# Local-attention blocks of 63 keys, v in one transfer a head, narrower pooling matmuls and pooled q and k on GpSimd

## The chip, the cores and the metric

The kernel runs on one core of one Trainium2 chip. The metric is device time in microseconds: the median of several executions. Before the change it is 880.45 us over 3 runs (879.81 to 880.62).

## The reference

Four batches of eight heads, 576 positions of 64 elements each, go through two attentions whose results are added: one over q, k and v averaged by fours (144 positions, its output repeated four times), and one on full resolution in which a position sees only the positions closer than 4. The sum is laid out as 2304 tokens of 512 and goes through two feed-forward layers of width 2048.

```
q_d, k_d, v_d = mean over groups of 4 positions
out_up  = repeat(softmax(q_d k_d^T / 8) v_d, 4)
mask    = |i - j| < 4
out_loc = softmax(where(mask, q k^T / 8, -1e9)) v
x = (out_up + out_loc) as (2304, 512)
h = x @ w_in;   x = (h * sigmoid(h)) @ w_out
h = x @ w_in2;  out = elu(h) @ w_out2
```

## The kernel before

All matmuls are float32 or pairs of rounded halves; a product of two matrices in the feed-forward layers is three matmuls (high by high, high by low, low by high).

The program has two stages. In the first, the attention of 16 head pairs (`attend`, a batch is four pairs) is interleaved with the first half of the first layer on blocks of 256 tokens (`unit`: lines 1124 and 1172). In the second (`paired`), the rest of both layers runs as matmuls of lines 1500, 1588 and 1590, with the instructions back to back on TensorE.

The order of the first stage is made by a planner in the program text: a `Job` has an engine, a planned duration, predecessors, buffers that it takes (`Slots`, `Hold`) and a due time; `pick` emits the job that can start earliest by the planner's clocks. The constants near line 56 (`D_LOCAL`, `S_LOCAL`, `STICK`, `T_FIRST`, `clock_of` and so on) are its prices. Every engine then executes its own list in that fixed order and waits on semaphores. Where the planner sees TensorE without work, `fill` puts in dummy matmuls (line 370).

For one head pair, `attend` does this. SyncE loads rows of q and k (line 604), TensorE turns them (line 653), ScalarE or VectorE copies them out (lines 681 to 687). Local attention takes ten blocks of 64 queries against 64 keys (line 773), masks, exponentiates and normalises them (`across`, on GpSimd line 784 or VectorE), turns them (line 900) and multiplies with v (line 1005). The windows of v come from `load_windows`: the first nine blocks start 57 rows apart and come in one transfer a head (line 614), the tenth starts at S - 64 and comes in a second (line 618). Pooled attention sums q and k by fours on VectorE (line 695), multiplies (line 847), exponentiates (line 869), normalises (line 886), turns (line 921) and multiplies with pooled v (line 939). Pooled v is made on TensorE for batch 0 (line 708, 22 matmuls a pair against a 0/1 matrix in `natv`), and for the other batches from another load of v (line 608) on GpSimd (lines 727, 728) or VectorE (line 732). Line 1022 adds both attentions into x.

The 16 weights of the first stage (8 slices of w_in, 8 of w_out, 512 KB each) come over SyncE's queue (lines 395, 400) into three buffers and one lent one. Each is decoded from its 64-bit input form on ScalarE (lines 426, 430) and VectorE (lines 434, 437, 441), and then split on ScalarE (line 1101) and GpSimd (line 1105). A buffer is free for the next weight when line 441 is done.

The last rows of the output are scaled and added on VectorE (line 1553) and stored by SyncE (line 1560).

Of the kernel before, what the change touches and what calls it, by code (L numbers as in the profile page):

```python
# [15 lines left out]
ALU = mybir.AluOpType  # L16
# [6 lines left out]
def attention_moe_moe2_kernel(ctx, tc, q, k, v, wi1, wo1, wi2, wo2, out):  # L23
# [32 lines left out]
    PACKED, PE_POOLED, HALVED, CHUNKED, STICK, T_SECOND = 0, 1, 0, 4, 3, 40.0  # L56
    STICK_FROM = 0
    BACKLOG = 3.0
    D_ROWS, D_LOCAL, D_V, D_W, S_ROWS, S_LOCAL, X_AFTER = 1.6, 1.9, 1.5, 2.2, 1.1, 2.2, 1
# [5 lines left out]
    SLACK, MOST_H, N_PSUM, SPLIT_F = 0.05, 2, 16, 3  # L65
    T_MM, T_FIRST, T_PAIR = 0.1185, 38.0, 6.4
# [10 lines left out]
    w0 = [57 * i for i in range(NW - 1)] + [S - WIN]  # L77
# [3 lines left out]
    for i in range(NW):  # L81
        lo, hi = a0[i], a0[i + 1] - 1
        assert q0[i] <= lo and hi < q0[i] + WIN
        assert w0[i] <= max(lo - 3, 0) and min(hi + 3, S - 1) < w0[i] + WIN
    WF_N, WS_N = 3, 3

    LENT = {'rows': [(5, 1), (6, 0), (6, 1)], 'ws': [(7, 0)], 'v': [(7, 1)]}
# [37 lines left out]
    def constants():  # L125
# [3 lines left out]
        for n, (half, low, high) in enumerate([(0, 0, 6), (0, -3, 3), (1, 0, 6), (1, -3, 3)]):  # L129

            for sign, bound in ((1, -low), (-1, high)):
                nc.gpsimd.affine_select(
                    out=tmp[:, n, :], in_=tmp[:, n, :], compare_op=ALU.is_ge, fill=MASKED,
                    base=bound + sign * WIN * half, pattern=[[sign, WIN]], channel_multiplier=-sign,
                )
        for s in range(NW // 2):
# [15 lines left out]
    clock_of = {"A": 0.0, "V": 4.0, "G": 4.0, "S": 0.0, "P": 5.0, "dma": 0.0, "port": 4.0}  # L152
# [357 lines left out]


    POOLED_BY = [(w, 0) for w in range(NW // 2 + 1)] + [(w, 1) for w in range(NW // 2, NW)]

    def pooler():
        return natv[:, :len(POOLED_BY) * HS].rearrange("p (n m) -> p n m", m=HS)

    def pool_matrix():

        m = pooler()
        nc.gpsimd.memset(m[:WIN], 1.0)  # L520
        for n0, n1 in ((0, NW // 2 + 1), (NW // 2 + 1, len(POOLED_BY) - 1), (len(POOLED_BY) - 1, len(POOLED_BY))):
            w, c = POOLED_BY[n0]
            x = m[:WIN, n0:n1]
            for sign, base_ in ((1, 0), (-1, FAC - 1)):
                nc.gpsimd.affine_select(
                    out=x, in_=x, compare_op=ALU.is_ge, fill=0.0, base=base_ + sign * (w0[w] - FAC * HS * c),
                    pattern=[[sign * w0[1], n1 - n0], [-sign * FAC, HS]], channel_multiplier=sign,
                )
        nc.vector.tensor_copy(m[WIN:P], m[:WIN])

    def pool_rows(w):

        return min(w0[1], w0[w + 1] - w0[w]) if w < NW - 1 else WIN
# [15 lines left out]
    )  # L549
    QKD0 = Slots([xb[:, c, :2 * SD] for c in range(NPAIR)])  # L550
# [28 lines left out]
    def attend(i, due):  # L579
# [5 lines left out]
        by_pe = b < PE_POOLED  # L585
# [24 lines left out]
        def load_windows():  # L610
            vw = hw.tile.rearrange("p (n d) -> p n d", d=D)
            for j in range(2):
                rows = v[b, h0 + j]
                nc.sync.dma_start(
                    vw[j * WIN:(j + 1) * WIN, :NW - 1, :],
                    bass.AP(tensor=rows.tensor, offset=rows.offset, ap=[[D, WIN], [w0[1] * D, NW - 1], [1, D]]),
                )
                nc.sync.dma_start(vw[j * WIN:(j + 1) * WIN, NW - 1, :], rows[w0[-1]:w0[-1] + WIN, :])
# [21 lines left out]
        copies = []  # L640
        prior = []
        for n_, cells in enumerate(([(0, c) for c in range(NTB - 1)], [(1, c) for c in range(NTB - 1)], [(0, NTB - 1), (1, NTB - 1)])):
# [21 lines left out]
            for which in range(2):  # L664
                n = TB * sum(w == which for w, _ in cells)
                if n:
# [17 lines left out]
                    else:  # L684
# [3 lines left out]
                        )  # L688
                    copies.append(alike(0.19 + 0.0008 * n, ops[0], 0.15 + 0.00106 * n, ops[1], [pj], uses=[bank]))
# [3 lines left out]
        def pool_qk():  # L693
            for which, src in enumerate(hqk.tile):
                nc.vector.reduce_sum(hqkD.tile[:, which * SD:(which + 1) * SD], src.rearrange("p (m r) -> p m r", r=FAC), axis=AX.X)

        red = Job("V", 1.48, pool_qk, copies, takes=[hqkD], uses=[hqk])
        vd = lambda: hvd.tile.rearrange("p (n d) -> p n d", n=4)
        pv = []
        if by_pe:  # L700
            bankv = [Hold(banks, "a") for _ in range(2)]

            def pool_v():
                vw = hw.tile.rearrange("p (n d) -> p n d", d=D)
                for n, (w, c) in enumerate(POOLED_BY):
                    for j in range(2):
                        rows_ = slice(j * WIN, j * WIN + pool_rows(w))
                        nc.tensor.matmul(  # L708
                            bankv[j].tile[:HS, c * D:(c + 1) * D], pooler()[rows_, n, :], vw[rows_, w, :],
                            start=n == 0, stop=n == len(POOLED_BY) - 1, skip_group_check=True,  # L710
                        )

            psv = Job("P", 0.85, pool_v, [lw], lat=0.2, takes=bankv, uses=[hw, hpool], mode="d")
            for j in range(2):
                dst = lambda j=j: hvd.tile[:HS, 2 * j * D:2 * (j + 1) * D]
                pv.append(alike(
                    0.29, lambda dst=dst, j=j: nc.scalar.copy(dst(), bankv[j].tile[:HS, :2 * D]),
                    0.29, lambda dst=dst, j=j: nc.vector.tensor_copy(dst(), bankv[j].tile[:HS, :2 * D]),
                    [psv], takes=[hvd] if j == 0 else [], uses=[bankv[j]],
                ))  # L720
            pv[1].after(pv[:1])
# [31 lines left out]
        for part, (s0, s1, halves_, outs) in enumerate(parts):  # L753
# [6 lines left out]
            def scores(s0=s0, s1=s1, held=held):  # L760
# [9 lines left out]
                for w in range(2 * s0, 2 * s1):  # L770
                    o, c = (w % 2) * WIN, (w // 2 - s0) * WIN
                    for j in range(2):
                        nc.tensor.matmul(  # L773
                            held[j].tile[o:o + WIN, c:c + WIN],
                            qT[j * D:(j + 1) * D, q0[w]:q0[w] + WIN],
# [979 lines left out]
```

## Time and profile before

| | |
|---|---|
| median of 3 runs | 880.45 us |
| profiled execution | 879.63 us |
| its span | 877.9 us |
| TensorE busy (matmuls) | 865.9 us, 99% |
| VectorE | 668.7 us, 76% |
| ScalarE | 543.7 us, 62% |
| GpSimd | 251.5 us, 29% |
| bytes moved | 100.08 MB, mean 114 GB/s |

The span is what the profile covers; the execution's own time is 1.7 us longer. Busy shares are means over two unlike stages, so the stages are read apart.

### The profile page before, as it was taken

How to read it: one execution, taken by the hardware profiler on the slowest of the kernel's cores; microseconds unless marked ns; L12 is line 12 of the kernel's file. 1: busy time of each engine (PE TensorE's matmuls, PEld its weight loads, DVE VectorE, ACT ScalarE, POOL GpSimd, SP SyncE). 2: the span in 40 equal slices, each digit the busy share in tenths (PEclk: the TensorE clock that was granted, in tenths of full speed). 3: DMA queues.
4: the chain of work that ended last, by engine and by line, in shares of the span. 5: the costliest groups of instructions: out<-in, count | busy, mean ns of one | idle time of the engine just before them, and what ended most of it. 6: DMA issues, size and time to landing. Idle time of an engine off the chain costs nothing.

```text
span 877.9 us, 17291 instructions
## 1 busy us (share of the span) xinstructions
PE 865.9 (99%) x6632; PEld 809.7 (92%) x6640; DVE 668.7 (76%) x1255; ACT 543.7 (62%) x1228; POOL 251.5 (29%) x269
## 2 busy tenths in 40 slices
PE   8989999999999999999999999999999999999998
PEld 5779989999999999999999998898998998998986
DVE  8888777776968988979569879389489797493552
ACT  5787675564568568466377387385586684561750
POOL 4488786664103011301024213010141041010000
PEclk9989999999999999999999999999999999999999
DMA  9996377612123436253521340541420531310301
GB/s 170 205 219 173 81 202 180 169 49 97 56 90 121 132 103 221 77 173 125 178 92 52 109 156 1 166 123 60 132 72 37 174 126 37 111 70 37 108 0 72
DMA packets 105522, 100.08 MB, mean 114 GB/s; under 512 B 62240, under 2 KB 92448, under 8 KB 105312
## 3 DMA queue, kind: packets, MB, share of 16 engines
q1 hardware_dynamic: 103072, 98.39, 38.1%
q8 instruction: 52, 0.85, 0.4%
q10 hardware_dynamic: 2368, 0.59, 0.4%
q14 instruction: 30, 0.25, 0.1%
HBM read 75.37 MB, written 23.59 MB: 113 GB/s over the span
## 4 chain that ended last, share of the span: by engine, by line
PE 94%; DVE 2%; DMA 2%; issue 1%; ACT 0%; SPq 0%; POOL 0%; ACTq 0%; POOLq 0%; DVEq 0%
PE b L1500 33%; PE b L1590 22%; PE b L1588 15%; PE b L1172 8%; PE b L1124 7%; PE b L653 1%; PE b L1005 1%; PE b L921 1%; PE b L939 1%; PE b L900 1%; PE b L773 1%; PE b L847 1%; PE b L708 1%; DMA rows<-in_k_dram 1%; DMA ws<-in_moe_w_out_dram 1%; DMA rows<-in_q_dram 1%
## 5 line engine op out<-in xcount | busy, mean ns | idle before, releaser
L1590 PE MATMUL b<-w,grw 128*128 128x512 f32 x384 | 121.2, 389 | 0.0
L1590 PE MATMUL b<-w,ghk 128*128 128x512 f32 x288 | 99.1, 389 | 0.0
L1500 PE MATMUL b<-xhr,xaw 128*128 128x384 f32 x360 | 96.4, 335 | 0.0
L1588 PE MATMUL b<-grw,w 128*128 128x384 f32 x352 | 91.2, 334 | 0.0
L1590 PEld LDWEIGHTS b<-w,grw 128*128 128x128 f32 x384 | 72.1, 188 | 14.9
L1500 PE MATMUL b<-xhr,w 128*128 128x384 f32 x320 | 83.8, 335 | 0.0
L1124 PE MATMUL b<-xh,w 128*128 128x256 f32 x384 | 82.5, 293 | 1.2 <-DVE t L1153 0.7
L1172 PE MATMUL b<-gh,w 128*128 128x256 f32 x384 | 79.6, 288 | 0.0
L1590 PE MATMUL b<-w,glk 128*128 128x512 f32 x192 | 74.8, 389 | 0.0
L1588 PE MATMUL b<-ghk,w 128*128 128x384 f32 x248 | 71.6, 334 | 0.0
L1124 PEld LDWEIGHTS b<-xh,w 128*128 128x128 f32 x384 | 64.7, 194 | 3.0 <-DVE t L1153 0.9
L1500 PE MATMUL b<-xlr,xaw 128*128 128x384 f32 x200 | 66.9, 334 | 0.0
L1500 PEld LDWEIGHTS b<-xhr,xaw 128*128 128x128 f32 x360 | 65.5, 188 | 0.0
L1590 PEld LDWEIGHTS b<-w,ghk 128*128 128x128 f32 x288 | 54.1, 188 | 11.1
L1172 PEld LDWEIGHTS b<-gh,w 128*128 128x128 f32 x384 | 63.3, 191 | 0.7 <-ACT t L1152 0.2
L1588 PEld LDWEIGHTS b<-grw,w 128*128 128x128 f32 x352 | 63.7, 188 | 0.0
L1512 ACT COPY hg<-b 128x384 f32<-128x384 f32 x60 | 28.7, 480 | 52.5 <-PE b L1500 51.9
L1553 DVE SCALAR_TENSOR_TENSOR part<-b,part 128x384 f32<-128x384 f32 (+1 forms) x42 | 25.0, 609 | 44.8 <-PE b L1590 28.4
L1283 DVE TENSOR_TENSOR xlr<-tail,xhr 128x768 fp32r<-128x768 f32 x51 | 49.6, 973 | 11.5 <-ACT xhr L1280 11.2
L1500 PEld LDWEIGHTS b<-xhr,w 128*128 128x128 f32 x320 | 58.0, 188 | 0.2
L1588 PE MATMUL b<-glk,w 128*128 128x384 f32 x168 | 56.1, 334 | 0.0
L1280 ACT CAST xhr<-tail 128x768 fp32r<-128x768 f32 x60 | 50.0, 834 | 7.0 <-DVE tail L1361 4.3
(259 smaller groups left out, 2380.8 us busy)
## 6 DMA issues: line engine op xcount, KB each, us to landing
ws<-in_moe_w_in_dram SPq DMA_DIRECT2D x32, 512.0 KB
ws<-in_moe_w_out_dram SPq DMA_DIRECT2D x31, 512.0 KB
tail<-x SPq DMA_DIRECT2D x24, 384.0 KB
x<-part SPq DMA_DIRECT2D x6, 768.0 KB
out_dram<-part SPq DMA_DIRECT2D x18, 256.0 KB
vw<-in_v_dram SPq DMA_DIRECT2D x28, 144.0 KB
tail<-xd SPq DMA_DIRECT2D x10, 384.0 KB
natv<-in_v_dram SPq DMA_DIRECT2D x22, 144.0 KB
```

The lines of the kernel that those rows point to most:

```text
L653: nc.tensor.transpose(bank.tile[:, n * TB:(n + 1) * TB], row(which, c)[:TB], ident[:TB, :TB])
L708: nc.tensor.matmul(bankv[j].tile[:HS, c * D:(c + 1) * D], pooler()[rows_, n, :], vw[rows_, w, :], start=n == 0, stop=n == len(POOLED_BY) - ...
L773: nc.tensor.matmul(held[j].tile[o:o + WIN, c:c + WIN], qT[j * D:(j + 1) * D, q0[w]:q0[w] + WIN], kT[j * D:(j + 1) * D, w0[w]:w0[w] + WIN], ...
L1124: nc.tensor.matmul(ph.tile[:, :NB0], w[a][:, c, :], x_slot(n, c, b_), start=start and m == 0, stop=stop and m == len(products) - 1,)
L1172: nc.tensor.matmul(y[d // 2].tile[:, o:o + NB0], w[m // 2][:, sl], gg(m % 2), start=f == 0 and m == 0 and d % 2 == 0, stop=fin and m == 2, ...
L1280: a = Job("A", ACT_[width], lambda: nc.scalar.copy(hi(), src), preds, gate)
L1283: other=("V", VEC_[width], lambda: nc.vector.tensor_tensor(lo(), src, hi().bitcast(F32), ALU.subtract)),
L1500: nc.tensor.matmul(acc_, a[:, cs], b[:, c, :], start=fresh and c == 0 and m == 0, stop=c == 1 and m == 2, skip_group_check=True,)
L1512: snap[after, j] = [Job("A", ACT_[NB], lambda dst=dst, acc_=acc_: nc.scalar.copy(dst, acc_), [], gate, due=soon)]
L1553: nc.vector.scalar_tensor_tensor(dst, src, sc, dst, op0=ALU.mult, op1=ALU.add)
L1588: nc.tensor.matmul(y[d][:, :NB], wm[:, sl], gm, start=first, stop=last_)
L1590: nc.tensor.matmul(y[d], gm[:, sl], wm, start=first, stop=last_)
```

## The change

A block of local attention now counts 63 keys (it had 64), and all ten blocks start 57 rows apart, so that v comes in one transfer a head. The last block has 63 key columns; its 64th score column is masked, and in batches 1 to 3 a matmul of one column more per head fills it. The 0/1 matrix for pooling v becomes 128 by 128, with v as the weights: ten matmuls a head with 14 to 16 columns, one copy, two transposes and one copy. It is used for the first seven pairs and not four. For batch 0, q and k are summed by fours in two additions each (`pool_twice`), for which the planner may take GpSimd or VectorE. The lent row buffers go. The very last output block is computed, scaled and stored in two halves of 256 columns, the second store from ScalarE's queue. Several planner constants change.

```diff
-    PACKED, PE_POOLED, HALVED, CHUNKED, STICK, T_SECOND = 0, 1, 0, 4, 3, 40.0
+    PACKED, PE_POOLED, HALVED, CHUNKED, STICK, T_SECOND = 0, 7, 0, 4, 2, 40.0
-    D_ROWS, D_LOCAL, D_V, D_W, S_ROWS, S_LOCAL, X_AFTER = 1.6, 1.9, 1.5, 2.2, 1.1, 2.2, 1
+    POOL_G = 1
+    D_ROWS, D_LOCAL, D_V, D_W, S_ROWS, S_LOCAL, X_AFTER = 1.6, 2.5, 1.9, 2.7, 1.1, 1.3, 1
-    SLACK, MOST_H, N_PSUM, SPLIT_F = 0.05, 2, 16, 3
-    T_MM, T_FIRST, T_PAIR = 0.1185, 38.0, 6.4
+    SLACK, MOST_H, N_PSUM, SPLIT_F = 0.05, 3, 16, 3
+    T_MM, T_FIRST, T_PAIR = 0.1185, 36.0, 6.4
-    w0 = [57 * i for i in range(NW - 1)] + [S - WIN]
+    KEYS = WIN - 1
+    w0 = [(KEYS - 6) * i for i in range(NW)]
-    LENT = {'rows': [(5, 1), (6, 0), (6, 1)], 'ws': [(7, 0)], 'v': [(7, 1)]}
+    LENT = {'ws': [(7, 0)], 'v': [(7, 1)]}
...
-    clock_of = {"A": 0.0, "V": 4.0, "G": 4.0, "S": 0.0, "P": 5.0, "dma": 0.0, "port": 4.0}
+    clock_of = {"A": 0.0, "V": 4.0, "G": 4.0, "S": 0.0, "P": 3.0, "dma": 0.0, "port": 4.0}
...
-        by_pe = b < PE_POOLED
+        by_pe = i < PE_POOLED
...
                 nc.sync.dma_start(
-                    vw[j * WIN:(j + 1) * WIN, :NW - 1, :],
-                    bass.AP(tensor=rows.tensor, offset=rows.offset, ap=[[D, WIN], [w0[1] * D, NW - 1], [1, D]]),
+                    vw[j * WIN:j * WIN + KEYS],
+                    bass.AP(tensor=rows.tensor, offset=rows.offset, ap=[[D, KEYS], [w0[1] * D, NW], [1, D]]),
                 )
-                nc.sync.dma_start(vw[j * WIN:(j + 1) * WIN, NW - 1, :], rows[w0[-1]:w0[-1] + WIN, :])
...
+        def pool_twice(which):
+            x = hqk.tile[which].rearrange("p (m r) -> p m r", r=FAC)
+            z = half_sums[which].rearrange("p (m r) -> p m r", r=2)
+            nc.gpsimd.tensor_tensor(z, x[:, :, 0:2], x[:, :, 2:4], ALU.add)
+            nc.gpsimd.tensor_tensor(
+                hqkD.tile[:, which * SD:(which + 1) * SD].rearrange("p (m o) -> p m o", o=1), z[:, :, 0:1], z[:, :, 1:2], ALU.add
+            )
...
-                for n, (w, c) in enumerate(POOLED_BY):
+                for w in range(NW):
+                    m0, m1 = pg[w], pg[w + 1]
                     for j in range(2):
-                        rows_ = slice(j * WIN, j * WIN + pool_rows(w))
                         nc.tensor.matmul(
-                            bankv[j].tile[:HS, c * D:(c + 1) * D], pooler()[rows_, n, :], vw[rows_, w, :],
-                            start=n == 0, stop=n == len(POOLED_BY) - 1, skip_group_check=True,
+                            bankv.tile[j * D:(j + 1) * D, m0:m1], vw[j * WIN:j * WIN + KEYS, w, :],
+                            pooler[j * WIN:j * WIN + KEYS, j, FAC * m0 - w0[w], :m1 - m0], start=True, stop=True, skip_group_check=True,
                         )
...
+            def turn_v():
+                for c in range(2):
+                    nc.tensor.transpose(bankt.tile[:HS, c * P:(c + 1) * P], hvt.tile[:, c * HS:(c + 1) * HS], ident)
...
+                        if final and k == FP - 1 and d == ny - 1:
+                            for c0, queue in ((0, nc.sync), (DM // 2, nc.scalar)):
...
-            prepare(i, dues[pos] - 2.5 if which == 0 else dues[pos + LAG] - 2.5)
+            prepare(i, dues[pos] - 4.0 if which == 0 else dues[pos + LAG] - 4.0)
```

The lists of the engines change in many places. Two of them matter here. The first is SyncE's list from the end of the loads of v windows for batch 0 on (`vw` and `yo` are buffers of windows, `ws` and `lent` of weights, `nat` and `lent` of q, k and v rows). Before:

```order
L614 DMA yo<-in_v_dram 64x9x64
L618 DMA yo<-in_v_dram 64x64
L400 DMA ws<-in_moe_w_out_dram 128x1024
L395 DMA ws<-in_moe_w_in_dram 128x4x256
L400 DMA lent<-in_moe_w_out_dram 128x1024
L604 DMA lent<-in_q_dram 96x6x64 x2
L604 DMA lent<-in_k_dram 96x6x64 x2
L608 DMA lent<-in_v_dram 72x512 x2
L395 DMA ws<-in_moe_w_in_dram 128x4x256
```

and with the change, from the first weight on:

```order
L399 DMA ws<-in_moe_w_in_dram 128x4x256
L609 DMA vw_116<-in_v_dram 63x10x64 x2
L609 DMA vw_117<-in_v_dram 63x10x64 x2
L609 DMA yo<-in_v_dram 63x10x64 x4
L404 DMA ws<-in_moe_w_out_dram 128x1024
L399 DMA ws<-in_moe_w_in_dram 128x4x256
L404 DMA lent<-in_moe_w_out_dram 128x1024
L399 DMA ws<-in_moe_w_in_dram 128x4x256
L599 DMA nat_113<-in_q_dram 96x6x64 x2
L599 DMA nat_114<-in_k_dram 96x6x64 x2
```

Eight transfers of v windows stand where sixteen stood, the fifth weight (the third w_in) has moved ahead of the rows of pair 4, and no load of v (line 608) stands here any more.

The second is GpSimd's list after it has built its constants (`ring` and `yo` hold scores, `tail` and `xa` turned q and k, `xb` their sums). Before, up to the first split of a weight:

```order
L784 TENSOR_TENSOR ring_118<-ring_118,small 128x640
L886 TENSOR_TENSOR ring_120<-ring_120,small 72x576
L784 TENSOR_TENSOR ring_119<-ring_119,small 128x640
L886 TENSOR_TENSOR yo<-yo,small 72x576
L784 TENSOR_TENSOR yo<-yo,small 128x640
```

and with the change, its start:

```order
L694 TENSOR_TENSOR natv<-tail 128x288
L695 TENSOR_TENSOR xb<-natv 128x144
L807 TENSOR_TENSOR ring_118<-ring_118,small 128x640
L909 TENSOR_TENSOR ring_120<-ring_120,small 72x576
L694 TENSOR_TENSOR natv<-xa 128x288
L695 TENSOR_TENSOR xb<-natv 128x144
L807 TENSOR_TENSOR ring_119<-ring_119,small 128x640
```

The two rows of line 694 and 695 stand four times ahead of the first normalisation (q and k of pairs 0 and 1), twice between pair 0's and pair 1's, and twice more for pair 3: all eight sums of batch 0 are on GpSimd, in line with the normalisations.

## Rows read from the trace of the kernel before

**Rows 1.** Stretches of 20 us: busy time (count) by engine, TensorE clock, DMA share, GB/s.
```profile
0.00:20.00 20.00, 17.60 (x243) 11.42 (x248) 16.32 (x43) 11.25 (x36) 8.46 (x27) 1.00 1.04 178
40.00:60.00 20.00, 17.57 (x255) 15.05 (x256) 17.60 (x37) 16.14 (x43) 14.21 (x17) 0.83 0.89 190
80.00:100.00 20.00, 20.00 (x209) 19.18 (x207) 15.24 (x30) 14.55 (x39) 12.86 (x15) 1.00 0.37 107
```
**Rows 2.** Waits of TensorE: line and what it waited for, us in total, times, longest.
```profile
PE b L370 <- issue: 2.0, 3, 1.6
PE b L653 <- DMA nat<-in_q_dram: 1.9, 2, 1.6
PE b L1124 <- DVE t L1153: 0.7, 1, 0.7
PE b L1124 <- DVE wf L441: 0.5, 1, 0.5
```
**Rows 3.** Stretches of 1 us, columns as in rows 1.
```profile
53.00:54.00 1.00, 1.00 (x26) 0.78 (x28) 1.00 (x2) 0.96 (x5) 0.90 (x3) 0.50 1.11 333
59.00:60.00 1.00, 1.00 (x10) 0.95 (x9) 0.90 (x6) 1.00 (x3) 0.73 (x1) 0.87 0.57 141
```
**Rows 4.** Chain that ended last, in order of time: start us, us, what.
```profile
258.50 23.97 PE b L1500 x138
872.98 2.05 DVE part L1553 x3
```
**Rows 5.** TensorE in order of time: start us, us, line, tiles, count [idle before <-releaser].
```profile
1.39 3.92 PE L370 MATMUL b<-t 128*128 128x512 bf16 x10 [1.39 <-DVE t L1614]
5.67 0.60 PE L653 MATMUL b<-ident,nat 96*128 96x96 f32 x5 [0.36 <-DMA nat<-in_q_dram]
6.11 1.03 PE L370 MATMUL b<-t 128*128 128x512 bf16 x4
9.28 0.75 PE L773 MATMUL b<-tail 64*64 64x64 f32 x40
12.98 1.21 PE L653 MATMUL b<-ident,rows 96*128 96x96 f32 x12
28.67 1.65 PE L708 MATMUL b<-yo,natv 57*72 57x64 f32 x44
63.29 0.28 PE L1124 MATMUL b<-xh,w 128*128 128x256 f32 x1
```
**Rows 6.** SyncE's queue in order of time.
```profile
11.68 0.73 SPq L614 DMA_DIRECT2D vw<-in_v_dram  x1
24.12 0.64 SPq L618 DMA_DIRECT2D yo<-in_v_dram  x1
25.43 0.43 SPq L395 DMA_DIRECT2D ws<-in_moe_w_in_dram  x1
873.70 1.69 SPq L1560 DMA_DIRECT2D out_dram<-part  x3
```
**Rows 7.** VectorE in order of time.
```profile
8.54 1.41 DVE L695 TENSOR_REDUCE xb<-tail 128x144 f32<-128x576 f32 x2
49.76 0.41 DVE L1153 SCALAR_TENSOR_TENSOR t<-t,b 128x256 f32<-128x256 f32 x1
57.33 0.69 DVE L441 SCALAR_TENSOR_TENSOR wf<-ws,b 128x512 int32<-128x512 int32 x1
```
**Rows 8.** GpSimd groups with shapes: count | busy us, mean ns of one | idle before.
```profile
L784 POOL TENSOR_TENSOR ring<-ring,small 128x640 f32<-128x640 f32 x27 | 34.0, 1260 | 29.1 <-DVE small L879 13.9 <-DVE small L830 8.2 <-DVE small L816 7.0
L728 POOL TENSOR_TENSOR vd<-natv 72x128 f32<-72x128 f32 x17 | 7.8, 457 | 2.1 <-PE b L939 0.9
L1070 POOL TENSOR_TENSOR xl<-xa,xh 128x256 fp32r<-128x256 f32 x16 | 11.5, 731 | 1.3 <-ACT xh L1066 1.3
```

**Rows 9.** GpSimd in order of time.
```profile
30.85 1.15 POOL L886 TENSOR_TENSOR ring<-ring,small 72x576 f32<-72x576 f32 x1 [2.25 <-DVE small L880]
```
**Rows 10.** DMA over 0 to 80 us in 40 slices of 2 us.
```profile
GB/s 6 219 202 213 214 215 216 260 133 105 86 119 135 227 383 299 203 221 204 172 166 135 143 232 262 193 291 143 225 112 321 223 274 224 173 224 207 134 134 322
```

## What was predicted

> **What bounds the kernel now.** I read the stretches of time first, then the waits of TensorE, the chain that ended last, and then each engine's list in order of time over the first 66 us. From 80 us on TensorE is busy in every stretch, and the chain is a run of back-to-back matmuls from 258.50 to 872.98 [rows 1, 4]. Those 614.5 us are the same matmuls after the change, so only three things can move: the start, the work that the first stage gives TensorE, and the end. In the start the reader should see TensorE 2.4 us short of each of two 20 us stretches, with VectorE at 16.3 and 17.6 of 20 [rows 1]; waits for rows of q (1.9 us), for issue (2.0), for a decoded weight (0.5) and for a VectorE result (0.7) [rows 2]; and seven slices, 53 to 60 us, in which the granted clock is between 0.50 and 0.87, so at the lower level of 1.2 GHz for most of them, after TensorE had waited for q at 50.7 to 52.3 [rows 2, 3]. The last of the four first-layer units of batch 0 that I take as a milestone (48 matmuls of line 1124) ends at 63.4 [rows 5]. From there to 258.50 are **195.1 us** in which TensorE hardly waits. The question is when the changed kernel passes the same milestone, and how much work it then has left.
>
> **TensorE's work.** The old pooling of v is 22 matmuls in 1.57 us, 0.071 each; 88 of them are 6.3 us [rows 5]. The new one is 140 matmuls of at most 16 columns and 14 transposes. No row shows such a matmul: it should be no dearer than the 20 of 64 columns in 0.75 us, 0.037 each [rows 5], and can't be cheaper than nothing. I take 0.037, because both load 64 by 64 weights each time. A transpose takes at most 1.21/12 = 0.10, or 0.12 at 128 columns. That is 5.2 + 1.7 = 6.9 us: as much as before, now over seven pairs. Batches 1 to 3 get 24 single-column score matmuls, 0.9 us by the same price (bounds 0 and 0.9).
>
> In the two lists the stretch ahead of the milestone differs. The changed one has 19 transposes, 18 score matmuls and 7 flips fewer ahead of it: 19 x 0.10 + 18 x 0.037 + 7 x 0.09 = 3.2 us that come later. Behind it also come 40 narrow matmuls with 4 transposes (2.0) and 22 single columns (0.8). So **6.0 us** more are left at the milestone, and the changed kernel breaks even if it passes it at 63.4 - 6.0 = **57.4**.
>
> **SyncE.** The 16 transfers of v windows hold its queue from 11.68 to 24.76, 0.8 us each, and the third weight goes out at 25.43 [rows 6]. In that time the DMA engines fall from some 215 GB/s to 86 to 135 [rows 10], so it is the issuing that is slow, and not the moving. Eight transfers end at about 18.3, and three weights start 6.5 us earlier. Behind them the third w_in now stands ahead of pair 4's rows and waits for the first decode to free a buffer. The loads of v for pairs 4 to 6 are gone, 3 x 288 KB.
>
> **VectorE.** From 8.54 to 49.76, its first instruction for the first layer, it hardly idles [rows 1, 7]: it paces the start. It loses four pairs of sums (4 x 1.41 = 5.6 us [rows 7]), the copy of the 0/1 matrix and half a pair's sum of v; it gains a few evictions. Before, the sixth weight leaves VectorE at 58.0 [rows 7]. In the changed list I add up the durations of the same instructions ahead of the sixth: from the first scores at about 11 us it is paced by GpSimd until some 24, and from there it runs without a gap for 25 us. The sixth weight is then done at about 49 and the seventh at 53.
>
> **GpSimd, and what it costs.** On TensorE nine more dummy matmuls stand ahead of the first transposes. Four of them take 0.86 us at the full clock [rows 5], so nine take 1.9; with the wait of 0.36 that they fill, the first transposes start at 7.2 and not 5.67, and the first scores 1.4 us later than 9.28 [rows 5]. The sums then go to GpSimd. From 256 elements (731 ns) to 640 (1260 ns) an addition costs 1.38 ns an element, so 288 elements are 0.78 us, and 144 are 0.46 to 0.48 [rows 8]: **1.25 us a sum, 10.0 us for eight**, 2.5 a pair where VectorE took 1.41. This is longer for each pair, and in line with the normalisations of 1.26 and 1.15 [rows 8, 9]. From 9.8 us, eight sums, three normalisations of either kind take until 27.0, and I put 27.5. TensorE waits for this list in its own order: pooled scores of pairs 0 and 1 stand ahead of the scores of pairs 1 and 2, and come about 2.5 and 1.4 us later than before. But by pair 2 the gain shows: its pooled normalisation ended at 32.0 [rows 9] and now ends at 27.5, because VectorE no longer delays what it needs.
>
> Additions that read every second pair of four elements are in no row of before. The bounds are the contiguous rows (1.25 us a sum) and twice that. I take the first: the pieces read are two adjacent elements, and the nearest rows are the same operation on the same engine. The middle, 1.88, is the first rival below. The Trainium skill (GPSIMD Engine Reference, Performance pitfalls for Q7 kernels) has a rule that speaks for that middle: an SBUF read whose step times element size exceeds 8 bytes takes about half as long again. Whether an outer step of 16 bytes counts for it, no run here shows.
>
> **The milestone.** TensorE's own list up to it is 36.0 us of work by the prices above and 47 dummies: ten in 3.9 us and 37 at 0.215, 8.0 [rows 5]. With the first 1.39 us that is a floor of **49.3**. The ceiling is that floor with all waits of rows 2 (5.1) and the half clock's 3.4 us (seven us at half speed) [rows 2, 3] coming back: **57.8**. The fifth weight, which the milestone needs, leaves VectorE at some 47.5, and the cast and GpSimd's split take another 2; 12 matmuls with flips among them follow. I take **52.5**, nearer to the weight than to the ceiling. The stall at 50.7 should go, as pair 5's rows are issued at about 40 and land by 48.
>
> **The end.** The last block's scaling is 0.69 us for 512 columns and about 0.41 for 256 [rows 7], which saves 0.27; the last store, from 875.39 to the span's end at 877.9 [rows 6], is half as large, which saves between nothing and 0.6. I take 0.5 in all (bounds 0 and 0.9).
>
> **The sum.** 52.5 + 195.1 + 6.0 = 253.6 for 258.5: -4.9. With the end, -5.4. The profiled execution took 879.63, so 874.2; it lies 0.8 under the median of the runs, to which I put **875.0**. The floor of the milestone gives 871.8, with the most that the end can give 871.4; the ceiling gives 880.4.
>
> **The rivals.**
> - *The sums are dear on GpSimd.* Midway between the bounds a sum takes 1.88 us; 8 x 0.63 = 5.0 us more in GpSimd's line, all of it on the way to pairs 2 and 3. The milestone moves to 57.5, and only the end is won: **880.0**, no change. For it: every sum reads with a step of four. Against: the other operands here are contiguous in pairs.
> - *Half of it.* SyncE's and GpSimd's gains do not add, because a weight still waits for one of three buffers; the milestone comes at 55: **877.5**. For it: two weights of the first five are issued only after a decode. Against: VectorE's list is shorter in either case.
> - *Slower: rows of q and k come late.* The change gives back the lent row buffers and puts weights ahead of pairs 4 and 5 in SyncE's list, where each weight waits for a decode. If pair 5's rows land after some 49.5, TensorE stands again, and the clock falls as at 53 us. Each such stall costs 1.6 us and 3.4 at half clock [rows 2, 3]; at pairs 4 and 5 both, 10 us, the milestone is at 62.5: **885.0**. For it: TensorE's list is fixed and the margin is about 2 us. Against: fifteen dummies stand in that stretch, and pair 4's rows go out at about 29.
> - *The change does not do what it says*: the planner could have left the sums on VectorE. The list excludes that: all eight are on GpSimd.
>
> **How the numbers follow.** The forecast has 0.60, the sums' rival 0.14, the half gain 0.12, the late rows 0.14. The range leaves out the late rows and the last of the floor: 871.4 to 880.8. A measurement of this kernel can tell about 0.2%, 1.8 us, from no change. Faster is the forecast and the half gain, 0.72; the same is the sums' rival, 0.14; slower the late rows, 0.14.
>
> **What would show it.** SyncE should issue the third weight before 20 us; the pooled sums should take 1.25 us each (1.9 is the first rival); the sixth decode should be done by 50; the matmuls of the second stage should start near 253.6; no slice between 45 and 62 should have a clock of 0.50. I am wrong if TensorE waits for rows of q or k after 40 us, or if the milestone lies after 57.4.

## The result and the profile after

The changed kernel takes **885.96 us** (median of 11 runs, 884.71 to 886.63) against 879.81 us of the kernel before on the same chip (11 runs, 878.09 to 885.99): a ratio of 1.0063, interval 1.0045 to 1.0081. It is slower by some 6 us where 5 us less were forecast. The profiled execution took 884.71 us, its span is 883.0 us, against 877.9 before. It is the fastest of the 11, 1.25 us under their median (0.18 before), so of the 6.2 us between the medians the two profiles hold 5.1; where the other executions spent the rest, no trace shows.

The 5.1 us between the spans lie in three places: 3.9 ahead of the first matmul of the second stage, 0.9 between it and the end of the matmuls in the chain that ended last, and 0.35 in the end behind that. The first matmul of the second stage, before and after:

```profile
247.41 0.34 PE L1500 MATMUL b<-xhr,w 128*128 128x384 f32 x1
251.29 0.34 PE L1523 MATMUL b<-xhr,w 128*128 128x384 f32 x1
```

The 258.50 of the prediction [rows 4] is a place 11 us further on, where the chain's row begins; in the changed kernel that place comes at 262.2, where 253.6 was forecast.

The start did what was forecast of it, in kind. Here are the same stretches of 20 us as in [rows 1]:

```profile
0.00:20.00 20.00, 17.55 (x222) 11.52 (x226) 12.05 (x39) 10.50 (x34) 12.65 (x36) 1.00 1.00 175
40.00:60.00 20.00, 19.25 (x286) 16.33 (x286) 19.38 (x40) 18.16 (x47) 14.90 (x16) 1.00 0.77 183
80.00:100.00 20.00, 19.00 (x229) 17.78 (x229) 16.91 (x32) 14.84 (x37) 10.43 (x10) 1.00 0.43 103
```

TensorE is busy 19.25 us of 40 to 60 where it was 17.57, the granted clock is 1.00 and not 0.83, and VectorE has 4.3 us less in the first 20. But 80 to 100 is no longer full. TensorE's waits, against [rows 2]:

```profile
PE b L923 <- DVE small L902: 0.6, 1, 0.6
PE b L647 <- DVE xa L1045: 0.5, 1, 0.5
PE b L944 <- DVE ring L932: 0.5, 1, 0.5
PE b L870 <- POOL xb L695: 0.4, 1, 0.4
```

No wait for rows of q or k is left and none for issue; in their place are many short ones for VectorE, GpSimd and ScalarE. TensorE in order of time, against [rows 5] (line 374 is the dummies, 647 the turning of rows, 721 the new narrow pooling, 1147 the first layer; line 735, further down, turns pooled v):

```profile
1.38 5.79 PE L374 MATMUL b<-t 128*128 128x512 bf16 x19 [1.38 <-DVE t L1660]
7.00 0.58 PE L647 MATMUL b<-ident,nat 96*128 96x96 f32 x5
...
21.81 1.34 PE L721 MATMUL b<-natv,vw 63*64 63x15 f32 x40
...
55.49 0.28 PE L1147 MATMUL b<-xh,w 128*128 128x256 f32 x1
```

The 20 matmuls of a pair have two entries each, so they stand as x40. From 21.81 to the next instruction at 23.08 these are 1.27 us, **0.064 each** and not 0.037. The milestone (48 matmuls of the first layer) is passed at 55.6: 7.8 us earlier than before, and 1.8 before the break-even point that I had put. SyncE, against [rows 6]:

```profile
11.82 6.27 SPq L609 DMA_DIRECT2D vw<-in_v_dram  x4
18.13 5.47 SPq L609 DMA_DIRECT2D yo<-in_v_dram  x4
23.65 0.87 SPq L404 DMA_DIRECT2D ws<-in_moe_w_out_dram  x1
24.56 0.43 SPq L399 DMA_DIRECT2D ws<-in_moe_w_in_dram  x1
```

Eight transfers hold the queue for 11.7 us, 1.47 each, where 16 held it for 13.1 [rows 6]. The third weight goes out at 24.56, 0.9 earlier and not 6.5. GpSimd (694 and 695 are the two additions of a sum, 909 the pooled normalisation of pair 2, against [rows 9]):

```profile
9.69 0.66 POOL L694 TENSOR_TENSOR natv<-tail 128x288 f32<-128x288 f32 x1 [4.55 <-ACT tail L675]
10.44 0.43 POOL L695 TENSOR_TENSOR xb<-natv 128x144 f32<-128x144 f32 x1
...
28.77 1.14 POOL L909 TENSOR_TENSOR ring<-ring,small 72x576 f32<-72x576 f32 x1 [1.95 <-DVE small L903]
```

A sum is 1.1 us, and the normalisation ends at 29.9 (before 32.0). The sixth weight leaves VectorE at 53.2, before at 58.0 [rows 7]:

```profile
52.50 0.68 DVE L445 SCALAR_TENSOR_TENSOR wf<-ws,b 128x512 int32<-128x512 int32 x1
```

The end, in the chain of waits, against [rows 4]:

```profile
846.37 31.34 PE b L1636 x138
877.73 1.37 DVE part L1582 x2
879.12 0.42 DVE part L1573
```

So the gains at the start are there, and behind the milestone they are gone: from there to the second stage the changed kernel takes 195.7 us, the kernel before 184.0.

**A tally of TensorE ahead of the second stage.** TensorE's list up to the first matmul of the second stage, each group from its start to the start of the next, and waits of over 0.15 us behind the first instruction as idle time (us; the rest holds the 1.4 us ahead of that instruction):

| | second stage starts | idle | dummies | v pooled and turned | scores | rest |
|---|---|---|---|---|---|---|
| before | 247.41 | 6.49 | 11.23 | 6.32 | 12.18 | 211.19 |
| after | 251.29 | 4.07 | 12.61 | 10.68 | 13.01 | 210.92 |
| four pairs (e1) | 249.78 | 8.09 | 12.45 | 5.75 | 12.74 | 210.75 |
| pairs 4 to 6 left out (e5) | 251.32 | 6.02 | 12.78 | 7.68 | 13.02 | 211.82 |
| ten dummies (e7) | 250.50 | 3.95 | 11.35 | 10.67 | 13.02 | 211.51 |
| no narrow pooling (e13) | 249.28 | 7.13 | 11.87 | 4.47 | 13.05 | 212.76 |
| that and half the dummies (e15) | 248.31 | 8.87 | 8.17 | 4.69 | 13.08 | 213.50 |

A dummy matmul is a wait that the planner has written into the list. Idle time and dummies together, the **room** that other engines leave on TensorE, are 17.72 us before and 16.68 after. The sum is safer than its parts: the program before has 48 dummies and its trace records of 40, and in e13 and e15 there are 42 of 47 and 22 of 25. So all that VectorE and SyncE were relieved of is worth 1.0 us of room, and the change fills TensorE with 4.4 us of pooling and turning and 0.8 of scores more. The sum is the 3.9. What stays to be tested is whether that work is the loss, or whether it only stands where TensorE would wait.

### The profile page after: what moved, and what is told of

The parts are those of the page before. It is cut to its first block, busy times and chain, and to the rows that moved or that the text cites. A ratio compares the mean times of both kernels' runs of the same rounds, so it can differ in the third digit from the quotient of the medians.

```text
span 883.0 us, 17603 instructions
## 1 busy us (share of the span) xinstructions
PE 872.4 (99%) x6808; PEld 814.2 (92%) x6808; DVE 668.9 (76%) x1258; ACT 543.8 (62%) x1226; POOL 248.8 (28%) x267
## 4 chain that ended last, share of the span: by engine, by line
PE 58%; DVE 1%; DVEq 0%; issue 0%
PE b L1523 26%; PE b L1636 22%; PE b L1634 10%; DVE part L1582 0%; DVE w L1306 0%; DVE hgx L1421 0%; DVE raw L441 0%; DVE raw L445 0%; DVE b L1531 0%; DVE ghk L1306 0%; DVE hg L1421 0%; DVE part L1573 0%; DVEq L1796 0%
## 5 line engine op out<-in xcount | busy, mean ns | idle before, releaser
L1147 PE MATMUL b<-xh,w 128*128 128x256 f32 x384 | 80.4, 290 | 0.3 <-DVE xa L1045 0.3
L1195 PE MATMUL b<-gl,w 128*128 128x256 f32 x192 | 54.3, 283 | 0.0
```

The costliest lines, as they stand in the source:

```text
L1147: nc.tensor.matmul(ph.tile[:, :NB0], w[a][:, c, :], x_slot(n, c, b_), start=start and m == 0, stop=stop and m == len(products) - 1,)
L1195: nc.tensor.matmul(y[d // 2].tile[:, o:o + NB0], w[m // 2][:, sl], gg(m % 2), start=f == 0 and m == 0 and d % 2 == 0, stop=fin and m == 2, ...
```

## The experiments

**Fewer pairs, other forms of the pooling.** The first four runs change one part each, and let the planner write its lists anew.

```diff
-    PACKED, PE_POOLED, HALVED, CHUNKED, STICK, T_SECOND = 0, 7, 0, 4, 2, 40.0
+    PACKED, PE_POOLED, HALVED, CHUNKED, STICK, T_SECOND = 0, 4, 0, 4, 2, 40.0
```

> The changed kernel with v pooled on TensorE for four pairs instead of seven (the planner re-orders the lists). Theory A (the loss is TensorE's own work: a narrow pooling takes 1.27 us for its 20 matmuls and 0.2 for its two transposes, so three more pairs are 3 x 1.5 = 4.5 us in a stage that TensorE bounds): about 4.5 us faster than the changed kernel, 881.5 us. Rival B (the loss is late waits between 60 and 120 us, from the row buffers that are no longer lent): no faster, 885 to 887, since pooling on GpSimd brings back three loads of v. Rival C (the sums on GpSimd): unchanged, 886.

885.95 us, 1.0066 of before (1.0043 to 1.0089), not theory A's 881.5. The pooling and turning fall by 4.9 us and TensorE's idle time grows by 4.0. The longest of the waits that come, in order of time:

```profile
50.13 0.71 PE L870 MATMUL b<-qkD 64*72 64x144 f32 x8 [1.23 <-DVE qkD L689]
55.65 0.36 PE L1195 MATMUL b<-gh,w 128*128 128x256 f32 x1 [1.46 <-DVE wf L445]
58.95 0.39 PE L1147 MATMUL b<-xh,w 128*128 128x256 f32 x1 [0.90 <-DVE t L1176]
```

All three are VectorE's results; in the changed kernel the pooling of pairs 4 and 5 stands in this stretch. The second stage starts 1.5 us earlier; a wait of 1.3 us for a split weight behind it (0.6 in the changed kernel) and a longer end give 1.2 of that back.

The kernel before, with its own pooling for seven pairs:

```diff
-        by_pe = b < PE_POOLED
+        by_pe = i < 7
```

> The kernel before with its own wide pooling of v on TensorE for seven pairs instead of four, nothing else edited (the planner re-orders). Theory A: 3 x 1.57 = 4.7 us more TensorE work, 880 + 4.7 = 884.5 us. Rival D (taking the loads and sums of v of pairs 4 to 6 off DMA, GpSimd and VectorE is worth as much in the start as it costs TensorE): 880 or less.

888.5 us, 1.0103 (1.0073 to 1.0133): slower than either theory has it. For seven pairs the old form takes 11.62 us of TensorE, where the new one takes 10.68 with its turning, and the second stage starts at 257.92. But the profiled execution is the slowest of the four (891.31 us): it has a wait of 2.2 us for issue, as in [rows 2], and the lower clock from 37.9 to 44.7 us behind it.

The narrow form with four quarters of the array: windows 0 to 4 and 5 to 9 in turn into opposite halves of two PSUM banks, so that all four quarters come up in turn, as at line 773 [rows 5]. The form in the diff uses two quarters and one bank.

```diff
-                for w in range(NW):
+                for w in (i_ + t * NW // 2 for i_ in range(NW // 2) for t in range(2)):
...
-                            bankv.tile[j * D:(j + 1) * D, m0:m1],
+                            bankv[t].tile[p_:p_ + D, m0:m1],
```

> The changed kernel with the narrow pooling spread over all four 64 by 64 quadrants of the array (windows 0 to 4 and 5 to 9 in turn, two PSUM banks, two copies), still seven pairs. Theory A1 (a narrow matmul costs 0.064 because each quadrant comes up again after one other matmul, where line 796 and line 1028 use four in turn and take 0.037): 20 matmuls in 0.75 us instead of 1.27, 7 x 0.52 = 3.6 us less, 882.3 us. Rival A2 (0.064 is what loading 63 by 64 weights and a matmul of 15 columns costs wherever it lies): 1.27 us again, 886 us.

```profile
22.34 0.77 PE L723 MATMUL b<-natv,vw 63*64 63x15 f32 x40
```

From 22.34 to the next instruction at 22.94 are 0.60 us; over seven pairs 140 matmuls take 5.16 us, 0.037 each. This is the price that I had forecast: **line 773's row, with four quarters and two banks, was the wrong row for the form in the diff**. Which of the two counts, the quarters or the banks, the run doesn't separate. The time is 894.08 us, 1.0162 (1.0134 to 1.019) all the same, since a second bank is taken and the planner's new lists hold TensorE up for 2.8 us (decoded weight) and 1.4 us (exponential); behind these waits the clock is at the lower level, for 13.6 us between 86 and 103, which are worth up to 6.8.

The sums back on VectorE:

```diff
-    POOL_G = 1
+    POOL_G = 0
```

> The changed kernel with pooled q and k of batch 0 on VectorE again (POOL_G 0; the planner re-orders). Theory A (the sums are not the cause, and their place is worth something to the milestone, which came 7.8 us earlier): slower than the changed kernel by 1 to 5 us, 887 to 891. Rival C (the sums in GpSimd's line cause the loss): faster, 881 to 884.

892.47 us, 1.0143 (1.0109 to 1.0177); milestone 67.3. With the lists written anew, the kernel with the sums on VectorE is some 6 us slower than the changed one, so the sums on GpSimd are not the cause of the loss. Part of the 6 us is the clock, which falls behind waits for VectorE at 52 to 56 us:

```profile
60.00:80.00 20.00, 20.00 (x217) 18.64 (x216) 11.72 (x26) 11.70 (x32) 9.95 (x11) 0.75 0.52 110
```

**With the lists kept.** New lists shift everything, so the following runs keep the order of each engine and change single instructions.

```diff
-                for w in range(NW):
+                for w in range(NW if b == 0 else 1):
```

> The changed kernel with every engine's list kept as it is, but for pairs 4 to 6 only the first of the ten windows is pooled on TensorE (the pooled v of these pairs is left out but for 16 columns). 54 of 140 narrow matmuls go, at 0.064 us each 3.4 us. Theory A (TensorE bounds the first stage, so its added work is the loss): 885.9 - 3.4 = 882.5 us. Rival (that work fills time in which TensorE would wait): 886.

886.38 us, 1.0073 (1.0042 to 1.0103); second stage at 251.32. Three us less work on TensorE returned nothing, as the rival has it. In order of time, with the remaining 4 of 40 at 47.61:

```profile
47.61 0.29 PE L721 MATMUL b<-natv,vw 63*64 63x15 f32 x4
...
50.68 0.39 PE L1147 MATMUL b<-xl,w 128*128 128x256 f32 x1 [0.71 <-POOL xl L1093]
...
56.85 0.38 PE L1195 MATMUL b<-gh,w 128*128 128x256 f32 x1 [0.48 <-ACT ring L892]
57.59 0.39 PE L1195 MATMUL b<-gl,w 128*128 128x256 f32 x1 [0.35 <-POOL gl L1181]
```

In the changed kernel none of these three instructions waits: the 1.05 us of pair 4's pooling covered the first, those of pair 5 the other two.

```diff
-                for w in range(NW):
+                for w in [w for w in range(NW) for _ in range(2)]:
```

> The changed kernel with every list kept, and each of the 140 narrow matmuls issued twice in a row. Theory A: the 100 ahead of the first-layer units and the 40 behind cost 0.064 each again, 8.9 us, less the 1.8 us in which TensorE idles ahead of the milestone: 893 to 895 us. Rival (hidden behind VectorE in the start): only the 40 behind the milestone count, 888.5 us.

902.93 us, 1.0239 (1.0189 to 1.0288), far more than 140 x 0.064 = 9 us. The reason is another one, TensorE's row and then slices of 2 us:

```profile
21.89 2.51 PE L721 MATMUL b<-natv,vw 63*64 63x15 f32 x80
...
22.00:24.00 2.00, 2.00 (x72) 2.00 (x74) 2.00 (x5) 0.48 (x1) 1.94 (x3) 1.00 0.99 238
24.00:26.00 2.00, 2.00 (x58) 1.66 (x57) 0.70 (x2) 1.18 (x3) 0.64 (x2) 0.78 1.02 345
26.00:28.00 2.00, 2.00 (x15) 1.34 (x13) 0.61 (x3) 1.10 (x5) 1.18 (x1) 0.50 0.87 319
...
54.00:56.00 2.00, 2.00 (x9) 1.14 (x8) 1.90 (x5) 1.11 (x2) 1.60 (x2) 0.54 0.00 0
```

TensorE is busy throughout, yet the granted clock falls to the lower level of 1.2 GHz at about 25 us and stays there for 30 us. What stands ahead of the fall are 40 narrow matmuls without a gap, 2.51 us from 21.89. So the run can't price the work: 30 us at half the clock are worth up to 15 of the 21 us by which this execution (906.08) is longer than the changed kernel's.

```diff
-        filler(min(int((gap - 0.1) / 0.22), 40))
+        n = min(int((gap - 0.1) / 0.22), 40)
+        filler(n if first_fill else n - 9)
```

> The changed kernel with every list kept but nine dummy matmuls fewer ahead of the first transposes (10 as before, not 19). Theory A: the first transposes start at 5.7 and not 7.0 us, but GpSimd's line and the weights set the milestone, so 0.3 to 1.3 us faster: 884.6 to 885.6. Rival E (the dummies delay everything): the full 1.3 us, 884.6 or less. If the clock stays low longer: 886 to 888.

884.58 us, 1.0053 (1.003 to 1.0075), second stage at 250.50: 1.3 us of dummies less returned 0.8. Seven of the ten executions lie at 883.9 to 885.2, three at 888.8 to 890.1 with a mean clock of 0.992 to 0.993. The time, at 884.6, lies where both forecasts touch and can't tell them apart.

The kernel before with blocks of 63 keys and one transfer a head, nothing else:

```diff
-    w0 = [57 * i for i in range(NW - 1)] + [S - WIN]
+    KEYS = WIN - 1
+    w0 = [(KEYS - 6) * i for i in range(NW)]
```

> The kernel before with only the blocks of 63 keys and v in one transfer a head; planner constants and all lists as before but for the transfers and the 24 single-column score matmuls. Theory A: the eight transfers of 630 rows hold SyncE's queue for 1.47 us each, 11.8 us, against 13.1 for the sixteen, so the third weight starts about 1.2 us earlier, and 24 single-column matmuls cost 0.9 us: 879.5 to 881. Rival F (the third weight starts 6.5 us earlier as I had forecast): 875 to 878.

880.72 us, 1.0001 (0.9984 to 1.0018): no change, and within theory A's range. SyncE:

```profile
11.87 5.82 SPq L616 DMA_DIRECT2D vw<-in_v_dram  x4
17.73 4.44 SPq L616 DMA_DIRECT2D yo<-in_v_dram  x4
...
23.21 0.42 SPq L397 DMA_DIRECT2D ws<-in_moe_w_in_dram  x1
```

The third weight is 2.2 us earlier, the milestone 0.6, and the scores with their single columns cost 0.6 more: the second stage starts 0.4 later and nothing is won.

**What paces instead.** If it is VectorE (19.38 of 20 us busy in 40 to 60), taking work from it must help. In batches 1 to 3 the two pooled sums (0.74 us each) become copies:

```diff
-            red = Job("V", 1.48, lambda: [pool_one(which) for which in range(2)], copies, takes=[hqkD], uses=[hqk])
+            red = Job("V", 1.48, lambda: [nc.vector.tensor_copy(hqkD.tile[:, which * SD:(which + 1) * SD], hqk.tile[which][:, :SD]) for which in range(2)], copies, takes=[hqkD], uses=[hqk])
```

> VectorE's pooled sums of q and k of batches 1 to 3 are left out: a copy of the first 144 columns stands in their place (two of 0.74 us each become two copies of some 0.25), all lists unchanged otherwise. That takes about 1 us from VectorE at 48.4 and at 59.4 us, and 12 us over the first stage. Theory V (with TensorE's pooling hidden, VectorE and the chain of weights behind it pace 40 to 100 us): TensorE's waits after the milestone shrink by about 1 us, first second-stage matmul near 250.3. Theory T (TensorE's own work paces): it stays at 251.3 within 0.3.

> The same, and in addition the narrow pooling of pairs 4 to 6 is left out as in the run before (first window only), so TensorE has 3.0 us less and VectorE 1 us less per pair. If the two engines bound 40 to 100 us together, the two edits gain more than the sum of each alone: first second-stage matmul 248.5 to 249.5. If a third chain (GpSimd's splits of x and weights) paces, it stays above 250.5 and the waits name GpSimd.

886.58 us (1.0076, 1.0058 to 1.0093) and 886.57 us (1.0075, 1.0053 to 1.0098). Neither is faster than the changed kernel, but **the edit did not take the work away**: the 24 copies took 16.8 us in all, as much as the 24 sums in the changed kernel. The pair of sums at 59.43 there, and the pair of copies in its place in the first run:

```profile
59.43 1.38 DVE L689 TENSOR_REDUCE qkD<-tail 128x144 f32<-128x576 f32 x2
60.95 2.26 DVE L709 COPY qkD<-tail 128x144 f32<-128x144 f32 x2
```

At 48.39 it is 1.46 us for 1.40. Of the 24 copies 13 took 0.17 to 0.37 us and 11 took 0.78 to 3.54; each of these 11 ended 0.09 or 0.10 us behind the end of an instruction of GpSimd. So the two runs don't tell whether VectorE paces. The second stage starts at 253.14 in the first run, later than both theories have it: 0.6 us are lost ahead of the first transposes and 0.64 at "issue" at 30.6. The profiled execution of the second says nothing on its stretches, because TensorE stopped there in the middle of its narrow matmuls:

```profile
29.43 1.16 PE L721 MATMUL b<-natv,yo 63*64 63x15 f32 x33
31.70 0.24 PE L721 MATMUL b<-natv,yo 63*64 63x15 f32 x3 [1.11 <-issue]
```

and the clock was at 0.50 for ten slices of 1 us behind it, the first and the last:

```profile
33.00:34.00 1.00, 1.00 (x10) 0.61 (x7) 1.00 (x3) 0.65 (x3) 1.00 (x2) 0.50 0.97 323
...
42.00:43.00 1.00, 1.00 (x9) 0.97 (x6) 0.93 (x5) 0.33 (x2) 0.32 (x1) 0.50 0.00 0
```

The planner's prices for transfers and issues as before; then these, four pairs, and the old last block:

```diff
-    D_ROWS, D_LOCAL, D_V, D_W, S_ROWS, S_LOCAL, X_AFTER = 1.6, 2.5, 1.9, 2.7, 1.1, 1.3, 1
+    D_ROWS, D_LOCAL, D_V, D_W, S_ROWS, S_LOCAL, X_AFTER = 1.6, 1.9, 1.5, 2.2, 1.1, 2.2, 1
```

> The changed kernel with the planner's five transfer and issue costs of before (for SyncE's list). Theory L (the order that these numbers write is what loses behind the milestone): first second-stage matmul near 249.5, time near 883. If the costs are not it: 251.3 and 885.5 within 1 us.

> The same costs of before, narrow pooling for the four pairs of batch 0 only, and one last block and store as in the kernel before. TensorE has 4.9 us less pooling and turning than in the changed kernel. If order and work are the loss: first second-stage matmul 247.5 to 248.5, tail 0.35 shorter, time 879 to 881, level with the kernel before or 1 us under it. If the gain goes into waits as with four pairs alone, it stays above 249.5 and the time above 883.

891.21 us (1.012, 1.0088 to 1.0153) and 888.38 us (1.0097, 1.0066 to 1.0127). The second stage starts at 252.07 and 252.72: both miss, and neither beats the kernel before. Their executions had a mean granted clock of 0.986 to 0.998, the changed kernel's 0.999 to 1.0, so part of these times is the clock; in the profiled ones it was at the lower level from 56.6 to 60.0 us and from 57.1 to 63.9. The last block's old form, in the chain of the second:

```profile
846.93 31.34 PE b L1636 x138
878.27 0.02 issue
878.29 2.05 DVE part L1582 x3
```

From the end of the chain's matmuls to the span's end (883.9) are 5.6 us; in the changed kernel 5.3, in the kernel before 4.9, with four pairs and the new form 5.8. The two halves bring nothing that stands out of this spread.

**Nearly all of the new work out.** The last three runs put the two readings of the tally against each other: W, TensorE's work is the loss; C, other engines' chains are.

```diff
-                for w in range(NW):
+                for w in range(1):
```

> Narrow pooling cut to the first window of each head for all seven pairs (126 of 140 matmuls left out, so pooled v is wrong), all lists unchanged otherwise: TensorE has about 7.7 us less work, 4.5 of it before the milestone. W (work of TensorE paces): milestone near 51, first second-stage matmul 243.5 to 246, below the kernel before (247.4). C (other engines pace): milestone 54.5 or later, second stage after 249.5, and the idle time of TensorE grows by 5 us or more.

882.77 us, 1.0028 (1.0014 to 1.0043). Of 6.2 us taken out, 2.0 came back at the second stage (249.28) and 3.1 became idle time. W's range for the second stage is missed by 3.3 us; C's bounds are missed too, by 0.2 there, by 0.7 at the milestone (53.8) and by 1.9 in idle time. The stretch from 40 us:

```profile
40.00:60.00 20.00, 17.47 (x199) 14.21 (x193) 19.42 (x41) 17.47 (x46) 16.39 (x17) 1.00 0.89 213
```

TensorE's 17.47 is close to the 17.57 of the kernel before [rows 1], and VectorE is at 19.4 of 20.

```diff
-        filler(min(int((gap - 0.1) / 0.22), 40))
+        filler(min(int((gap - 0.1) / 0.22), 40) // 2)
```

> Each group of dummy matmuls behind the first nine halved, 22 fewer in all (some 5.3 us at 0.22 to 0.43 each), lists unchanged otherwise. W: as dummies are work like any other, the second stage starts 3 to 5 us earlier (246.5 to 248.5). C: dummies only fill waits; second stage 250.5 to 251.5, idle up by 4 to 5 us, and if the clock falls in the gaps, later than 252.

> Both edits (pooled v wrong as in the first): TensorE has 13 us less. W: second stage near 240. C: not before 248.5, TensorE idle for 15 us or more before the second stage, and VectorE, ScalarE and GpSimd named by the waits: their lists are then the time that no work on TensorE can beat.

Half the dummies alone: 888.43 us (1.0088, 1.0062 to 1.0114); its profiled execution stood for 2.2 us at "issue" at 29.3 and had half the clock behind it. At 28 us it was 1.1 ahead of the changed kernel. One of the four executions had a mean clock of 1.0: 884.90 us. Both edits: 881.38 us (1.0012, 0.9996 to 1.0028), second stage at 248.31. TensorE's waits there between 2 and 130 us, the longest:

```profile
PE b L923 <- POOL ring L807: 1.5, 3, 1.1
PE b L870 <- POOL xb L695: 0.8, 1, 0.8
PE b L923 <- DVE small L902: 0.8, 1, 0.8
```

With 10.4 us less on TensorE than in the changed kernel, the second stage comes 3.0 us earlier, still 0.9 later than before the change. W's 240 is missed by 8 us, C's 248.5 by 0.2 and its 15 us of idle time by 6. By what came back, C holds for about two thirds and W for one. TensorE's waits name no single engine.

**Where the third comes back.** With kept lists each matmul can be laid beside the same one of the changed kernel. How much later (+) or earlier (-) it starts, in us:

| start in the changed kernel | 7.00 | 36.22 | 50.09 | 50.91 | 251.29 |
|---|---|---|---|---|---|
| pairs 4 to 6 left out (e5) | +0.20 | +0.20 | -0.86 | +0.12 | +0.03 |
| no narrow pooling (e13) | +0.61 | -1.95 | -2.90 | -1.93 | -2.01 |
| that and half the dummies (e15) | +0.08 | -2.93 | -3.88 | -2.92 | -2.97 |

What is left out behind 36 us shows for a moment and is gone at the next wait; all that is won is won ahead of 36. There VectorE waits for TensorE. Its two longest waits between 20 and 36 us in the changed kernel, and then the stretch behind, in the changed kernel and in e13:

```profile
DVE natv L729 <- PE b L721: 1.0, 2, 0.7
DVE small L816 <- PE b L796: 0.9, 2, 0.7
```

```profile
36.00:60.00 24.00, 23.11 (x316) 18.55 (x308) 23.18 (x49) 21.36 (x58) 16.97 (x17) 1.00 0.74 168
36.00:60.00 24.00, 20.91 (x232) 16.11 (x232) 23.26 (x48) 20.94 (x53) 18.46 (x19) 1.00 0.80 188
```

In e13 the first of the two waits is gone and 0.2 us of the second is left. From 36 to 60 VectorE is busy for 23.2 of 24 us, with one wait over 0.15 us (0.3, for ScalarE), in the changed kernel and in all three of the table. So VectorE's list is the chain that fits: work on TensorE costs time where VectorE waits for it, and little where VectorE is full. This is read from traces; no run took work from VectorE there.

## Why the prediction was wrong

- **The step that failed first is the yardstick.** "52.5 + 195.1 + 6.0": I took the milestone as the measure of the start, and put the work left behind it at +6.0. It was passed at 55.6, and the work and waits behind it were +11.7. Of these, 5.6 are turns of q and k, scores and flips of scores (4.0 forecast), 3.1 pooling and turning of v (2.0), 1.5 idle time and 1.1 longer matmuls of the two layers (nothing for either). The earlier milestone is for the most part another order: of its 7.8 us, 4.9 are less time for turns, scores and flips ahead of it, and 5.6 more of them stand behind. Idle time and dummies, which no order hides, fell by 1.0 us only. Neither of the signs of being wrong that I had named came: neither looks at the work left behind the milestone.
- **Dummies were counted as work that stays**, in the floor of 49.3, and shown idle time as all that TensorE had to win. The kernel before had 11.2 us of dummies beside its 6.5 us of idle, the changed one 12.6. The change shortened that room by 1.0 us only, and of the work taken out in e13 and e15 two thirds did not come back: waits for GpSimd, VectorE and ScalarE stand in its place.
- **The price of a narrow matmul** was 0.037 from line 773's row, and is 0.062 over all 140 (8.62 us for 5.2). I gave "both load 64 by 64 weights each time" as the reason; with the same weights, in four quarters and two banks, e3 has 0.037. The 14 turns took 2.06 us for 1.7. Together +3.8 us against the forecast. By e13 about a third of such work is on the path, ahead of 36 us; the rest stands in the room.
- **SyncE**: "eight transfers end at about 18.3". I kept the time of a transfer and halved their number. One transfer of a whole head holds the queue for 1.47 us, two of before for 1.6, so the third weight came 0.9 us earlier for 6.5. What sets that time stays open: not the number of transfers alone, and not the rows alone, as before 576 rows took 0.73 us and 64 rows 0.64 [rows 6]. In the lists of the kernel before, e8 shows all of this part to be worth nothing.
- **VectorE**: the sixth weight at 53.2 for 49, with the same late weights and with GpSimd's list, which ended at 29.9 for 27.5. It was to run without a gap from 24 us on; up to 53 it waited for 2.7 us, 1.7 of them for TensorE.
- **The end**: -0.5 forecast, +0.35 measured. Behind the first matmul of the second stage the changed kernel loses 1.2 us in all, of which 0.6 is one wait of line 1634 for VectorE's split of a weight (line 1306). In e11 and e12, with the planner's transfer prices of before, that wait is gone; in e2, with the same prices, it is there, so it goes with the lists as they come out.
- **Right**: the sums on GpSimd (1.1 us for 1.25), so the first rival fell. 288 elements in 0.66 us are less than the contiguous row's estimate of 0.78. The Trainium skill's rule (GPSIMD Engine Reference, Performance pitfalls for Q7 kernels), by which these reads might take half as long again, does not show in that row; the page's remedy is to keep the inner step at 8 bytes or less, which these reads do (4 and 8 bytes). Right too: the stall at 50.7 and the half clock behind it are gone. (The ceiling gives 880.3 by the same sum, not 880.4.) The slower rival's time (885.0) is near the result by luck, as its mechanism did not happen: TensorE waits for no rows of q or k after 40 us.

What stays open is the cause of the whole 3.9 us ahead of the second stage. The pooling of pairs 4 to 6, the start's dummies and the planner's transfer prices were each taken away or put back, and none brought the second stage more than 1.5 us forward. VectorE's list is the likely chain from 36 to 60 us, but that is argued, and e9 and e10, meant to test it, left VectorE its work.

## What to carry to other kernels

Where a list is filled with dummies, add them to the idle time before asking what a faster engine can win, and compare kernels at a point at which both have done the same work. A price taken from the nearest row must share the form of what it prices: here, which quarters of the array and which PSUM banks small matmuls use in turn. When work is taken from one engine with the lists kept and its place fills with waits for others, it is not worth its own duration. And when an edit is to relieve an engine, read in the trace what the instructions put in its place took.

## What was not expected of the hardware

- Narrow matmuls that alternate between two quarters of the array, in one PSUM bank, took 0.064 us each (20 in 1.27 us); in four quarters and two banks 0.037 (140 in 5.16 us).
- A copy on VectorE from SBUF to SBUF (128x144) took 0.17 to 0.37 us 13 times and up to 3.54 us 11 times, then ending 0.09 or 0.10 us behind an instruction of GpSimd (e9). The sums of four times the input, in the same places, took 0.70 to 0.75 each time.
- 40 narrow matmuls in one piece kept TensorE busy in every slice, and the granted clock still fell to the lower level for 30 us (e6). A busy engine in the profile is no guarantee of the higher one.
- TensorE stood at "issue" for 0 to 2.2 us between 29 and 37 us, with lists that are the same up to there for different lengths: 0.64 and 1.11 us at the same instruction in e9 and e10. In e10 and e14 (2.2 us) the clock fell to 1.2 GHz for some ten us behind it, in e2 (2.2 us) for seven; in e9, and behind 1.6 us in the kernel before [rows 2], it did not. What decides that was not tried; a single profiled execution of these kernels can be several us off by it.
- SyncE's time for a transfer of v grew from 0.8 us, the mean of two a head, to 1.28 (e8) and 1.47 (changed kernel) when one carried the whole head.
